# Softcapped attention and a leaky two-matrix layer: weight norms in groups of four chunks, new priorities in the plan, and an exact statement of transposes

## Chip, core and metric

One core of a Trainium2 chip. The metric is the device time of one execution in microseconds, the median of several runs.

## What is computed

The inputs q, k and v have the shape (4, 12, 448, 64): batches, heads, positions, head size.

```python
scores = scale * q @ k^T                    # scale = 1 / sqrt(64)
scores = cap * tanh(scores / cap)           # cap = 30
attn   = softmax(scores)                    # over the last axis
x      = (attn @ v), heads side by side     # (1792, 768)
h      = x @ w_in                           # w_in (768, 2048)
g      = max(h, 0) + alpha * min(h, 0)      # alpha (2048)
out    = g @ w_out                          # w_out (2048, 768)
```

w_in and w_out come as 64-bit floats, the rest as 32-bit floats.

## The kernel before

Products of full precision are made from 16-bit pieces: a number is scaled by a power of two and split into a high and a low half, and three products (high-high, high-low, low-high) stand for one. Batch 0's attention works with 32-bit products instead, save its last unit.

**Attention.** Heads go in pairs, six pairs a batch. In batch 0 each pair is done in two units (parts of 192 and 256 of its 448 columns); in batches 1 to 3 a pair is one unit (`attention`): load q and k, take their absolute maximum (L693, then `allmax`, a transpose on TensorE, a maximum, and a broadcast back by TensorE), scale and split them (L703, L704), turn them by a DMA transpose (L709), then in blocks of 128 queries, two at a time (`steps`): products S (L724), tanh (L508), maximum (L513), exponent (L520), then scale and split the weights (L381 and L389 into `pw`, three buffers) and turn them by DMA transposes (`turn_split`, L547) into `ptall`, which has three slots for the heads, two of which a pair uses. The PV product (L597) follows, and its result goes to `xring` in eight slots, (6 * batch + pair) mod 8. Pairs 2 to 5 of batch 1 take the slots that batch 0's pairs had.

**Weights.** A matrix has 16 chunks of 128 x 768. A chunk is loaded (L825), converted from 64 to 32 bits by three VectorE operations (`to_f32`, L837, L841, L847) and its norms are taken: six products of the chunk with itself on TensorE (L861), whose maxima VectorE reduces (L866, written by L345 in the trace). `norms` does this for a group of `WG` chunks in one PSUM bank. For w_in, each group then gets its scale (`root2`: `allmax` over the group's columns, L358, L360, L362, L365, then L870, L873, L902), and its chunks are scaled and split (`split_w`). For w_out, the norms are taken by groups too, but one scale for all 16 chunks follows the last group.

**Products.** mm1 of a batch (L741) makes g for 16 chunks of w_in from all six pairs; for batch 0 in the two parts. mm2 (L782) makes the output. Evacuations of both go over ScalarE, VectorE and GpSimd (L381, L751, L375, L386).

**The order.** Nothing is issued as it is written. Every piece of work is given to a `Plan` with a priority, an estimate of its length on each engine that may do it, and the regions it reads and writes. `order` plays this forward in an estimated time: each engine that is free takes the ready item with the lowest priority number. The order that results is what is emitted; each engine then works through its own list in order, and waits on the chip for the true dependences. PSUM banks p0 to p3 are lent by kind: at most three for attention ("a"), three for mm1 and mm2 ("m"), and one for norms and `allmax` ("n"), from the first piece that uses a handle to the last. Where TensorE would stand idle before `FILL_END` of the planned time, the plan gives it a product on the identity whose result nobody reads (L991), which keeps its clock up. The constants at the top are the priorities: `A_S` for the units of batch 0, `B1_P` and `B_S` for the pairs of batches 1 to 3, `ST1_P` for a block of queries within one, `PV_P` for the PV product, `WI_P`, `WI_S`, `WO_P`, `WO_S` for the chunks of the weights (`LD_P`, `LO_P` for their loads), `WT_P`, `WT_S` for the scaling of w_out, `MM_P` for mm1, `EVAC_P` for evacuations. `PEN` and `PEN2` are what VectorE adds to the priority of an item that another engine could do.

Of the kernel before, what the change touches and what calls it, by code (L numbers as in the profile page):

```python
# [26 lines left out]
PD_B = 5  # L27
MQ = 3
AQ = 3
PEN = 422.47  # L30
PEN2 = 365.74
B0_P = -18.88
LD_P = -3.44
LO_P = -170.16
MM_P = 732.81
X_P = 22.66
ST_P = -8.0
ST1_P = 14.53
PV_P = 54.55
QK_P = 1.76  # L40
V_P = 31.8
WI_P = 37.0
WI_S = 4.06
A_S = 12.69
MM1_P = 0.51
WO_P = 95.27
WO_S = 3.65
WT_P = -69.69
WT_S = -13.16
B1_P = 65.06  # L50
B_S = 40.73
EVAC_P = 153.38
LAT = 200.0
START = 1230.0
WINDOW = 4096 / 1.2
FILLS = 1
WG = 2
XI = 1
XO = 1
AI = 1  # L60
# [1 line left out]
PW = 3  # L62
QA = 1.0
VA = 0.5
FILL_END = 398871.32
EXPONENT = 0x7F800000


# [7 lines left out]
class Plan:  # L76
# [15 lines left out]
    def op(self, prio, times, fn, r=(), w=(), rows=1.0, port=True):  # L92
        o = lambda: None
        o.prio, o.times, o.fn, o.rows, o.idx, o.port = prio, times, fn, rows, len(self.ops), port
        o.handles, deps = [], set()
        for write, regions in ((False, r), (True, w)):
            for x in regions:
                if isinstance(x, Handle):
                    if x not in o.handles:
                        o.handles.append(x)  # L100
                        x.ops.append(o)
                    x = (x, 0, 1)
                space, lo, hi = x
                old = self.acc.setdefault(space, [])
                deps.update(e[2] for e in old if e[0] < hi and lo < e[1] and (write or e[3]))
                if write:
                    old[:] = [e for e in old if e[0] < lo or hi < e[1]]
        for write, regions in ((False, r), (True, w)):
            for x in regions:
                space, lo, hi = (x, 0, 1) if isinstance(x, Handle) else x  # L110
                self.acc[space].append((lo, hi, o.idx, write))
        o.deps = len(deps)
        o.next = []
        for d in deps:
            self.ops[d].next.append(o)
        self.ops.append(o)
        return o

    def order(self):
# [32 lines left out]
        def put(o):  # L152
            for e in o.times:
                heapq.heappush(ready[e], (o.prio + ((PEN if "act" in o.times else PEN2) if len(o.times) > 1 and e == "dve" else 0.0), o.idx, o))

# [82 lines left out]
def kernel(  # L238
# [15 lines left out]
    NCH = 4  # L254
# [124 lines left out]
    def scaled(e, o, i, s):  # L379
        if e == "act":  # L380
            nc.scalar.activation(out=o, in_=i, func=AF.Copy, scale=s)  # L381
        else:
            nc.vector.tensor_scalar(out=o, in0=i, scalar1=s, scalar2=None, op0=ALU.mult)
# [14 lines left out]
    def load(prio, dst, src, b, pair, w):  # L398
        op(prio, {"sp": (500, 1900, 1000)}, lambda e: nc.sync.dma_start(out=dst.rearrange("p (h c) -> p h c", h=2),
                                                          in_=heads(src, b, pair)), w=w)  # L400
# [7 lines left out]
    def loads32():  # L408
        for pair in range(NPAIR):
            n = 2 * NCH * D  # L410
            for i, src in ((4, k), (6, q)):
                o = pair % 3 * n
                t = wpair[i + pair // 3].rearrange("p a b -> p (a b)")[:CP, o:o + n]
                raw32[i, pair] = t, (("wp", i + pair // 3), o, o + n)
                load(QK_P + A_S * pair, t, src, 0, pair, [raw32[i, pair][1]])
        vbatch(0)
# [11 lines left out]
    def vbatch(b):  # L428

        u = Unit()  # L430
        vb.append(u)
        t = vam[:, b % 2]
        u.vmx, u.inv, u.s = (t[:, NPAIR + i:NPAIR + i + 1] for i in range(3))
        u.osc, u.tok = small[:, 12 + b:13 + b], ("vam", b % 2)
        prio = V_P if b == 0 else B1_P + (b - 1) * NPAIR * B_S - B_S
        op(prio, {"dve": 30}, lambda e: nc.vector.memset(t[:, :NPAIR], 0.0), w=[(u.tok, 0, 9)])
        for pair in range(NPAIR):
            rv, m = vslot(b, pair)
            v0[b, pair] = rv, m
            load(prio + 0.4 * pair, rv, v, b, pair, [m])  # L440
            op(prio + 0.4 * pair, {"dve": 680}, lambda e, pair=pair, rv=rv: absmax(t[:CP, pair:pair + 1], rv),
               r=[m], w=[(u.tok, pair, pair + 1)], port=False)
        prio += 3
        op(prio, {"dve": 80}, lambda e: nc.vector.tensor_reduce(out=u.vmx, in_=t[:, :NPAIR], axis=AX.X, op=ALU.max),
           r=[(u.tok, 0, 6)], w=[(u.tok, 6, 7)])
        first, *rest = pow2(u.inv, u.s, None)
        allmax(prio, u.vmx, P, [(u.tok, 6, 7)], first, [(u.tok, 7, 9)])
        chain(prio, rest, w=[(u.tok, 7, 9)])
# [35 lines left out]
    def steps(u, prio, n, S_, s_ns, sr_, scale, dma):  # L484
# [3 lines left out]
        for i0 in range(0, nb, 2):  # L488
# [5 lines left out]
            sr = (("S", i % 2), 0, 1)  # L494
            pr = prio + (ST1_P if u.b else ST_P) * i0

# [40 lines left out]
    def turn_split(u, pr, n, c, t, tr, f, fr):  # L537

        w = pws[blk_no[0] % PW]
        wt = [(("pw", blk_no[0] % PW), z, z + 1) for z in range(2)]  # L540
        blk_no[0] += 1
        hi, lo = w[:, :NCH, :CP], w[:, NCH:, :CP]
        op(pr, {"act": 640, "dve": 470}, lambda e: scaled(e, hi, t, f), r=[*tr, fr], w=[wt[0]])
        op(pr, {"dve": 680}, lambda e: split_lo(lo, t, f, hi), r=[*tr, fr, wt[0]], w=[wt[1]])
        for h, rows, cols in spans(n, c):
            full = rows.stop - rows.start == P
            op(pr, {"sp": (1294, 1275, 896) if full else (1225, 1275, 448)}, lambda e, h=h, rows=rows, cols=cols: nc.sync.dma_start_transpose(  # L547
                out=u.pt[h][:, :, cols], in_=w[rows].rearrange("p g k -> p (g k)")),
               r=wt, w=[("pt", u.po[h] + 4 * cols.start, u.po[h] + 4 * cols.stop)])

    def turn_32(u, pr, n, c, t, tr, f, fr):

# [79 lines left out]
    def attention32(part, pair):  # L632
# [3 lines left out]
        o, n = PART[part]  # L636
        prio = A_S * (u.idx + 1) + B0_P * part
        ktr = ("tall", pair * S, (pair + 1) * S)
# [30 lines left out]
        if dma:  # L669
            h = PV_split(u, prio + X_P, n, *split_v(u, prio, vt, vr))  # L670
        else:
            h = PV_32(u, prio + X_P, n, vt, vr)
        if dma:
            xout(u, prio + X_P, h, n, o, 1 / P_TOP)
        else:
            xout(u, prio + X_P, h, n, o, vb[0].s, [(vb[0].tok, 7, 9)])


    def attention(b, pair):
        u = Unit()  # L680
        u.b, u.pair, u.idx = b, pair, unit_no[0]
        unit_no[0] += 1
        prio = B1_P + ((b - 1) * NPAIR + pair) * B_S
        n = 2 * NCH * D
# [42 lines left out]
        steps(u, prio, S, S_, lambda c: 430 if c == 3 else 380, [qt], [sc, amt], True)  # L727
        h = PV_split(u, prio + PV_P, S, vs, vt)
        xout(u, prio + PV_P, h, S, 0, 1 / P_TOP)

    grn = [0]

    def mm1(b, j, o, n, prio):
# [13 lines left out]
        grn[0] += 1  # L747
        pr = EVAC_P + prio * 1e-4
        sgt = [("sg", 0, 1)]
# [25 lines left out]
    def mm2(b, t, hf, prio):  # L775
# [10 lines left out]
        for part in range(4):  # L786
# [7 lines left out]
        osc = vb[b].osc if t < 3 else joint[:, b // 2:b // 2 + 1]  # L794
        op(EVAC_P + prio * 1e-4, either(NH, True), lambda e: scaled(e, osb[:, cols], ps_p[h.slot][:, :NH], osc),
           r=[h, *oscs], w=[osr], port=False)
# [6 lines left out]
        for rows in [out_rows(b, t * P, P)] if t < 3 else [out_rows(b - 1, 3 * P, QP), out_rows(b, 3 * P, QP)]:  # L803
            for t0, m, dst in rows:
                op(EVAC_P, {"sp": (500, 1100, 800)}, lambda e, p=p, m=m, dst=dst: nc.sync.dma_start(
                    out=dst[:, a], in_=osb[p:p + m, a]), r=[osr])
# [80 lines left out]
    def w_in_chunks(j0, n):  # L887

        flats = []
        for j in range(j0, j0 + n):  # L890
            prio = WI_P + WI_S * j
            if j + 2 < NF:
# [3 lines left out]
            flats.append((flat, fr))  # L896
            load_w(prio + LD_P, flat, fr, j % 4, src_wi(j), True)
            to_f32(prio, j % 4, flat, fr, share(j, XI))
# [7 lines left out]
    def w_out_all():  # L906
        for j in range(NF):
            prio = WO_P + WO_S * j
            load_w(prio + LO_P, room[j], room_r(j), WO_STAGE[j], src_wo(j), False)
            to_f32(prio, WO_STAGE[j], room[j], room_r(j), share(j, XO))  # L910
            if j % WG == WG - 1:
                js = range(j - WG + 1, j + 1)
                norms(prio, [(room[i], room_r(i)) for i in js], n_wo[:, js[0]:j + 1], ("n_wi", js[0], j + 1))
        root2(WT_P, s_wo, ("s_wo", 0, 1), n_wo, ("n_wi", 0, NF), [wo_scales])
        for j in range(NF):
            split_w(WT_P + WT_S * j, wo[j], room_r(wo_room[j]), room[j], room_r(j), s_wo[:, j:j + 1], ("s_wo", 0, 1), share(j, AO))

# [29 lines left out]
    def out_scale(b):  # L947
# [4 lines left out]

        op(WT_P + 1, {"dve": 150}, scale, r=[(vb[b].tok, 7, 9), ("s_wo", 0, 1)], w=[(("osc", b), 0, 1)])

    def mm1_batch(b, o, n, part):
        for j in range(NF):
            mm1(b, j, o, n, MM_P + 1000 * 2 * b + MM1_P + 10 * part + 0.1 * j)

# [7 lines left out]
    def all_ops():  # L966
        loads32()
        g_scales(30)
        for part in range(2):
            for pair in range(NPAIR):  # L970
                attention32(part, pair)
        for j in range(0, NF, WG):
            w_in_chunks(j, WG)
        for part in range(2):
# [17 lines left out]

    plan.fill, plan.fill_until = fill, FILL_END
    nc.sync.dma_start(out=capt, in_=cap.to_broadcast([P, 1]))
# [44 lines left out]
```

## Time and profile before

| | |
|---|---|
| median of 3 runs | 758.37 us (757.72 to 758.9) |
| profiled execution | 758.37 us, span 756.6 us |
| TensorE busy | 729.0 us, 96% |
| VectorE, ScalarE, GpSimd busy | 510.4, 452.1, 153.7 us |
| mean granted clock of TensorE | 0.988 |

The span goes from the first to the last instruction; the rest of the time lies around it. A granted clock of 1 is 2.4 GHz, of 0.5 is 1.2 GHz; a mean in between is a mixture of the two levels. Busy TensorE includes the fill products.

### The profile page before, as it was taken

To read this page: it belongs to the slowest core of one execution; us is meant where nothing else is said; L and a number is where in the kernel's file an instruction comes from. 1 tells how busy PE (TensorE), PEld (TensorE's weight loads), DVE (VectorE), ACT (ScalarE), POOL (GpSimd) and SP (SyncE) were. 2 spreads that over 40 slices of the span, in tenths; PEclk is the share of its full clock that TensorE was granted. 3 is DMA by queue.
4 is the path that set the end of the run, shared out by engine and by line. 5 is a ranking of instruction groups with operands and counts; after the bars stand their busy time and mean duration, and the time that the engine had idled before them with its cause. 6 is when DMAs were issued, how large, how long until landed. Compare 5 with 4: busy or idle time off the path is not lost.

```text
span 756.6 us, 13862 instructions
## 1 busy us (share of the span) xinstructions
PE 729.0 (96%) x5237; PEld 456.6 (60%) x5237; DVE 510.4 (67%) x1039; ACT 452.1 (60%) x897; POOL 153.7 (20%) x292
## 2 busy tenths in 40 slices
PE   9999999869899999999999999999999999999997
PEld 5766676658788655676545555555555555555664
DVE  3788899998877977777788777877887432443000
ACT  4768888845658966666685666777668531332010
POOL 1211112222344221121443210123343000000000
PEclk9999999987999999999999999999999999999999
DMA  8964545748875649999557799997755660000001
GB/s 204 279 182 130 160 130 139 208 131 200 187 128 98 108 106 203 180 189 171 110 90 143 153 185 191 194 176 144 126 119 96 127 119 1 22 1 1 21 22 42
DMA packets 227938, 98.70 MB, mean 130 GB/s; under 512 B 191456, under 2 KB 224160, under 8 KB 227872
## 3 DMA queue, kind: packets, MB, share of 16 engines
q1 hardware_dynamic: 227872, 97.82, 62.2%
q8 instruction: 41, 0.67, 0.4%
q14 instruction: 25, 0.20, 0.1%
HBM read 45.82 MB, written 5.51 MB: 68 GB/s over the span
## 4 chain that ended last, share of the span: by engine, by line
PE 52%; DMA 5%; DVE 1%; ACT 1%; issue 1%; SPq 0%; POOL 0%; ACTq 0%; DVEq 0%
PE p L741 22%; PE p L782 20%; PE s L724 4%; PE p L597 4%; DMA ptall<-pw 3%; DMA qkTs<-nat 2%; PE p L991 1%; DMA rqk<-in_k_dram 1%; DVE pw L389 0%; PE p L365 0%; SPq L547 0%; ACT nat L381 0%; DVE mxs L513 0%; ACT tall L520 0%; ACT tall L508 0%
## 5 line engine op out<-in xcount | busy, mean ns | idle before, releaser
L741 PE MATMUL p<-xring,wi 128*128 128x448 f16 (+2 forms) x1440 | 230.4, 320 | 5.8 <-DVE xring L389 3.9
L782 PE MATMUL p<-wp,gall 128*128 128x384 f16 x1344 | 225.2, 326 | 0.0
L741 PEld LDWEIGHTS <-wi 128*128 128x128 f16 x1440 | 138.4, 100 | 92.5 <-issue 10.2
L782 PEld LDWEIGHTS <-gall 128*128 128x128 f16 x1344 | 130.0, 98 | 89.6 <-issue 4.3
L520 ACT ACTIVATE tall<-tall,mxs,small 128x448 f32<-128x448 f32 x126 | 94.3, 750 | 17.6 <-POOL mxs L515 15.9
L389 DVE SCALAR_TENSOR_TENSOR pw<-tall,rr,pw 128x448 f16<-128x448 f32 x126 | 85.3, 689 | 19.1 <-ACT pw L381 18.7
L381 ACT ACTIVATE pw<-tall,rr 128x448 f16<-128x448 f32 x100 | 64.8, 662 | 55.6 <-DMA ptall<-pw 40.4
L515 POOL TENSOR_SCALAR mxs<-mxs,small 128x2 f32<-128x2 f32 (+1 forms) x93 | 48.0, 517 | 225.8 <-DVE mxs L513 190.1
L386 POOL TENSOR_TENSOR gall<-gr,gall 128x384 f16<-128x384 f32 (+4 forms) x80 | 64.6, 815 | 131.4 <-ACT gall L375 80.9
L751 DVE SCALAR_TENSOR_TENSOR gr<-p,ca_g,gr 128x448 f32<-128x448 f32 (+2 forms) x80 | 46.8, 585 | 46.0 <-ACT gr L381 45.4
L513 DVE TENSOR_REDUCE mxs<-tall 128x2 f32<-128x896 f32 (+1 forms) x72 | 68.7, 959 | 12.0 <-ACT tall L508 11.6
L508 ACT ACTIVATE tall<-s,ams 128x896 f32<-128x896 f32 (+1 forms) x72 | 64.5, 904 | 10.5 <-PE s L724 4.4
L724 PE MATMUL s<-qkTs 128*128 128x448 f16 (+1 forms) x288 | 60.0, 356 | 4.7 <-DMA qkTs<-nat 3.7
L381 ACT ACTIVATE gr<-p,cs_g 128x448 f32<-128x448 f32 (+2 forms) x54 | 28.8, 533 | 48.0 <-PE p L741 47.1
L375 ACT ACTIVATE gall<-gr 128x384 f16<-128x384 f32 (+4 forms) x83 | 34.8, 433 | 35.0 <-DVE gr L751 34.8
L525 POOL TENSOR_SCALAR rr<-sums 128x2 f32<-128x2 f32 (+1 forms) x96 | 30.2, 315 | 114.2 <-ACT tall L520 82.1
L381 ACT ACTIVATE wp<-p,small 128x384 f32<-128x384 f32 x21 | 12.2, 579 | 59.5 <-PE p L782 59.5
L597 PE MATMUL p<-ptall,vs 112*64 112x448 f16 (+1 forms) x456 | 46.2, 350 | 1.0 <-DMA ptall<-pw 1.0
L991 PE MATMUL p<-ident 128*128 128x128 f16 x695 | 43.2, 223 | 1.7 <-POOL ident masks.py:199 1.7
L991 PEld LDWEIGHTS <-ident 128*128 128x128 f16 x695 | 40.9, 100 | 4.1 <-POOL ident masks.py:199 1.7
L724 PEld LDWEIGHTS <-qkTs 128*128 128x128 f16 (+1 forms) x288 | 21.7, 100 | 28.1 <-issue 9.9
L666 PE MATMUL s<-tall,qkTs 128*128 128x448 f32 x84 | 35.8, 551 | 1.2 <-ACT gall L508 1.2
(141 smaller groups left out, 844.7 us busy)
## 6 DMA issues: line engine op xcount, KB each, us to landing
wp<-in_moe_w_in_dram SPq DMA_DIRECT2D x16, 768.0 KB, 4.9
wp<-in_moe_w_out_dram SPq DMA_DIRECT2D x16, 768.0 KB, 4.7
rvs<-in_v_dram SPq DMA_DIRECT2D x38, 224.0 KB, 3.2
rqk<-in_q_dram SPq DMA_DIRECT2D x18, 224.0 KB, 3.2
rqk<-in_k_dram SPq DMA_DIRECT2D x18, 224.0 KB, 3.5
ptall<-pw SPq DMA_TRANSPOSE x148, 3.3
wp<-in_k_dram SPq DMA_DIRECT2D x6, 224.0 KB, 7.8
wp<-in_q_dram SPq DMA_DIRECT2D x6, 224.0 KB, 7.7
```

Of the source, the lines that this page charges most:

```text
L381: nc.scalar.activation(out=o, in_=i, func=AF.Copy, scale=s)
L386: (nc.gpsimd if e == "pool" else nc.vector).tensor_tensor(out=o, in0=a, in1=b, op=ALU.subtract)
L389: nc.vector.scalar_tensor_tensor(out=o, in0=i, scalar=s, in1=hi, op0=ALU.mult, op1=ALU.subtract)
L508: op(pr, {"act": 245 + 377 * m}, lambda e, s=s, t=t, m=m: nc.scalar.activation(out=t, in_=s[:, :m, :S].rearrange("p c (j k) -> p c j k", j ...
L513: op(pr, {"dve": 136 + 469 * m}, lambda e, mt=mt, t=t: nc.vector.tensor_reduce(out=mt, in_=t, axis=AX.XY, op=ALU.max), r=tr, w=[mr], port= ...
L515: op(pr, {"dve": 200, "pool": 440}, lambda e, mt=mt: (nc.gpsimd if e == "pool" else nc.vector).tensor_scalar(out=mt, in0=mt, scalar1=ncap, ...
L520: nc.scalar.activation(out=t[:, x], in_=t[:, x], func=AF.Exp, scale=capt, bias=mt[:, x:x + 1], accum_out=u.sums[:, c:c + 1])
L597: nc.tensor.matmul(pv[x * D:(x + 1) * D, :n], vs[:, z, c:c + D], u.pt[x][:CP, y * NCH + kc], start=(i == 0), stop=(i == len(prods) - 1))
L724: nc.tensor.matmul(s[rows], qT[:, x * S + cols.start:x * S + cols.stop], qkT[:, r0:r0 + NCH, :], start=(z == 0), stop=(z == 1))
L741: nc.tensor.matmul(ps_p[h.slot][:, :n], w[:, z, kk, :], x[:, d, o:o + n], start=(kk == 0 and z == d), stop=(kk == NPAIR - 1 and z == 1))
L782: nc.tensor.matmul(ps_p[h.slot][:, :NH], g[j][:, d, t * P:(t + 1) * P], w[:, z, hf * NH:(hf + 1) * NH], start=(j == 0 and z == d), stop=(j ...
L991: nc.tensor.matmul(ps_p[slot][:, :P], ident.bitcast(F16)[:, :P], ident.bitcast(F16)[:, P:], start=True, stop=True)
```

## The change

`WG` goes from 2 to 4, so that `norms` and, for w_in, `root2` take four chunks at a time. The priorities get other values. In `turn_split`, the region that a DMA transpose writes is stated to the plan as the eight strips that it writes, where it was stated as one block of a head's region. `FILL_END` is lower.

```diff
--- before.py
+++ after.py
@@ -27,34 +27,34 @@
 PD_B = 5
 MQ = 3
 AQ = 3
-PEN = 422.47
-PEN2 = 365.74
-B0_P = -18.88
-LD_P = -3.44
-LO_P = -170.16
-MM_P = 732.81
-X_P = 22.66
-ST_P = -8.0
-ST1_P = 14.53
-PV_P = 54.55
-QK_P = 1.76
-V_P = 31.8
-WI_P = 37.0
-WI_S = 4.06
-A_S = 12.69
-MM1_P = 0.51
-WO_P = 95.27
-WO_S = 3.65
-WT_P = -69.69
-WT_S = -13.16
-B1_P = 65.06
-B_S = 40.73
-EVAC_P = 153.38
+PEN = 593.1
+PEN2 = 357.34
+B0_P = -21.6
+LD_P = -4.13
+LO_P = -146.94
+MM_P = 766.13
+X_P = 30.7
+ST_P = -12.3
+ST1_P = 9.3
+PV_P = 53.98
+QK_P = -5.54
+V_P = 27.5
+WI_P = 31.8
+WI_S = 4.16
+A_S = 12.4
+MM1_P = 6.26
+WO_P = 75.25
+WO_S = 5.62
+WT_P = -127.9
+WT_S = -15.47
+B1_P = 46.83
+B_S = 32.07
+EVAC_P = 201.2
 LAT = 200.0
 START = 1230.0
...
 FILLS = 1
-WG = 2
+WG = 4
 XI = 1
 XO = 1
 AI = 1
@@ -62,7 +62,7 @@
 PW = 3
 QA = 1.0
 VA = 0.5
-FILL_END = 398871.32
+FILL_END = 365429.37
 EXPONENT = 0x7F800000
 
 
@@ -546,7 +546,7 @@
             full = rows.stop - rows.start == P
             op(pr, {"sp": (1294, 1275, 896) if full else (1225, 1275, 448)}, lambda e, h=h, rows=rows, cols=cols: nc.sync.dma_start_transpose(
                 out=u.pt[h][:, :, cols], in_=w[rows].rearrange("p g k -> p (g k)")),
-               r=wt, w=[("pt", u.po[h] + 4 * cols.start, u.po[h] + 4 * cols.stop)])
+               r=wt, w=[("pt", u.po[h] + (g_ * n + cols.start) / 2, u.po[h] + (g_ * n + cols.stop) / 2) for g_ in range(2 * NCH)])
 
     def turn_32(u, pr, n, c, t, tr, f, fr):
 
```

## Rows read from the trace of the kernel before

**Rows 1.** Windows: from:to us, length, PE PEld DVE ACT POOL busy (xcount), PEclk, DMA, GB/s.
```profile
25.00:100.00 75.00, 73.72 (x525) 50.58 (x523) 61.78 (x129) 57.36 (x121) 10.85 (x28) 1.00 0.63 177
125.00:175.00 50.00, 37.35 (x316) 29.90 (x314) 46.79 (x91) 34.37 (x76) 11.51 (x21) 0.90 0.68 182
175.00:238.00 63.00, 60.26 (x563) 49.73 (x561) 48.77 (x99) 40.28 (x90) 25.20 (x38) 0.95 0.75 152
238.00:250.50 12.50, 12.50 (x196) 11.07 (x196) 11.10 (x25) 11.03 (x20) 4.38 (x4) 1.00 0.53 103
250.50:314.80 64.30, 62.81 (x406) 35.80 (x404) 50.33 (x94) 47.00 (x85) 11.07 (x23) 1.00 0.80 151
314.80:348.70 33.90, 32.79 (x490) 27.93 (x489) 26.00 (x61) 22.14 (x44) 7.22 (x14) 1.00 1.09 192
348.70:642.00 293.30, 292.13 (x1784) 157.06 (x1782) 206.52 (x412) 183.58 (x359) 72.20 (x138) 1.00 0.72 133
```

**Rows 2.** The same view of the fill products alone (L991); the sum is of all stretches.
```profile
238.00:250.50 12.50, 9.66 (x167) 9.41 (x168) 1.00 0.53 103
...
314.80:348.70 33.90, 24.57 (x418) 23.67 (x417) 1.00 1.09 192
348.70:642.00 293.30, 0.16 (x3) 0.00 (x0) 1.00 0.72 133
...
sum 756.60, PE 43.17 PEld 40.89; mean PE 4.32 PEld 4.09
```

**Rows 3.** The chain that ended last: start us, us, what.
```profile
332.83 0.31 PE p L365 x2
...
343.68 2.39 PE p L597 x24
...
348.86 3.40 PE p L741 x18
...
353.02 0.10 PE p L362
```

**Rows 4.** Groups of instructions: line, engine, operation, shapes, count, busy us, mean ns, idle before.
```profile
L513 DVE TENSOR_REDUCE mxs<-tall 128x2 f32<-128x896 f32 x54 | 57.9, 1077 | 10.8 <-ACT tall L508 10.5
...
L847 DVE SCALAR_TENSOR_TENSOR wp<-wp,wp 128x768 int32<-128x768 int32 x18 | 17.2, 959 | 0.0
...
L513 DVE TENSOR_REDUCE mxs<-tall 128x1 f32<-128x448 f32 x18 | 10.9, 606 | 1.2 <-ACT tall L508 1.1
...
L837 DVE TENSOR_SCALAR wp<-wp 128x768 int32<-128x768 int32 x18 | 9.8, 545 | 1.8 <-DMA wp<-in_moe_w_out_dram 1.8
...
L360 DVE TENSOR_SCALAR mxt<-ident,mxt 2x2 f32<-2x2 f32 x26 | 7.8, 299 | 0.9
...
L345 DVE TENSOR_REDUCE n_wi<-p 128x2 f32<-128x256 f32 x16 | 6.7, 418 | 4.4 <-PE p L861 4.4
...
L358 DVE TENSOR_REDUCE mxt<-p 2x1 f32<-2x128 f32 x8 | 2.2, 276 | 3.0 <-PE p L362 3.0
...
L873 DVE TENSOR_SCALAR iv_wi<-iv_wi 128x2 f32<-128x2 f32 x8 | 1.2, 156 | 0.0
```

**Rows 5.** TensorE in order of time: start us, us, instruction.
```profile
175.26 0.85 PE L861 MATMUL p<-wp 128*128 128x128 bf16 x6
...
189.78 0.52 PE L861 MATMUL p<-wp 128*128 128x128 bf16 x6
...
195.88 0.26 PE L362 MATMUL p<-ident,small 112*2 112x112 f32 x1
...
216.67 0.51 PE L861 MATMUL p<-wp 128*128 128x128 bf16 x6
...
232.75 0.51 PE L861 MATMUL p<-wp 128*128 128x128 bf16 x6
```

**Rows 6.** TensorE's longest wait, 100 to 350 us: us in total, times, longest.
```profile
PE p L741 <- DVE xring L389: 3.9, 1, 3.9
```

**Rows 7.** Waits of SyncE's queue, 180 to 230 us: us in total, times, longest.
```profile
SPq L547 <- DVE gr L751: 11.8, 3, 5.3
```

## Prediction

> **What bounds the kernel now.** Read first the busy times by stretch, cut where TensorE's work changes [rows 1]. TensorE is busy for 729.0 us of the 756.6 us span, but this is not 729.0 us of wanted work: 43.17 us are fill products on the identity, which the plan puts in where it finds TensorE free [rows 2]. What is left, 685.9 us, is the floor that no order of the work can go under, give or take what the clock costs. So the question for any new order is how much of the 27.6 us of idle and of the 43.2 us of fills it can remove. The rows of the fills and of the stretches say where these are: 12.65 us of plain idle at 125 to 175 us, where the granted clock also falls to 0.90 in the mean; 9.66 us of fills at 238 to 250.5; 24.57 us of fills at 314.8 to 348.7. After that TensorE is full: 292.13 of 293.30 us up to 642 us, with 0.16 us of fills. Everything that can be won lies ahead of 348.7 us.
>
> Then the chain of waits says what ends the last hole [rows 3]. The first product of mm1 of batch 1 starts at 348.86 us. Just ahead of it stands the last PV product of batch 1's attention (343.68 us) with fills on either side. mm1 reads all six pairs' columns, so it waits for the last pair. Behind it TensorE never waits again, so each microsecond by which batch 1's attention ends earlier is a microsecond off the end, until the holes are used up. The hole at 238 to 250.5 has another cause: mm1 of batch 0 is done and w_out isn't scaled yet.
>
> What is late in batch 1's attention? From 175 to 348.7 us VectorE is busy for 48.77 + 11.10 + 50.33 + 26.00 = 136.2 of 173.7 us, a share of 0.784, ScalarE for less [rows 1]. In 125 to 175 us VectorE has 46.79 of 50, a share of 0.936. So there VectorE is the bound, and what goes first on it matters; later the pairs wait for one another (a pair of heads takes two of three slots of transposed weights, and pairs 2 to 5 may write their columns only after mm1 of batch 0 has read the old ones). A pair that comes to 175 us further along loses less there.
>
> **The change part by part.**
> *Groups of four.* For w_in, 8 groups become 4. Each group that goes takes with it a maximum over a transposed column (276 ns), the diagonal (299), and three small VectorE operations on its columns, of which one is shown (156 each) [rows 4]: 1.04 us. Four groups: 4.2 us of VectorE. The reductions of the norms halve in number and double in width. None of 512 columns from PSUM was run; the nearest rows are the 448- and 896-wide maxima, 606 and 1077 ns, so 1.05 ns for a column more; 256 columns more make 418 + 269 = 687 ns. At the least it costs nothing more (418), at the most twice (836). With 687, 8 x 418 - 4 x 687 = 0.6 us is saved for w_in, and as much for w_out. In all 5.4 us of VectorE's 510.4 us. On TensorE a group takes a transpose and a broadcast, 0.10 and 0.31 us of its time by the chain [rows 3]; four of them are 1.6 us. They fall at 25 to 125 us, where TensorE has little left (73.72 of 75 us at 25 to 100). I take 1.6 us there as the gain of this edit (bounds 0, if the plan only puts fills in its place, and 5.4, if all of VectorE's part counted), and don't add VectorE's: most of it falls ahead of the stretch in which VectorE is full.
>
> *What the group delays.* The first chunk of a group now waits for three others before it is scaled. A chunk takes one conversion step of 545 ns and two of about 959 on VectorE [rows 4], 2.5 us, so two more chunks are 5 us of VectorE and more where other work comes between. For w_out this is nothing: the one scale of all sixteen chunks waits for the last chunk either way. For w_in it costs nothing as long as mm1 reaches a chunk later than that, since the product over part 0 stands behind all attention products in priority; without this cover it is 5 us a group, once.
>
> *The bank.* A group keeps its PSUM bank from its first product to its reduction, and only one such handle may be live; the maxima of the attention's q and k use the same kind. By the norm products of w_out, six a chunk, the second last four chunks lie at 175.26 to 189.78 us and the last four at 216.67 to 232.75 (the first and last of each four are shown) [rows 5], so a hold would be 14.5 and 16.1 us instead of the length of a pair. The only q and k maximum near them, at 195.88 us, falls between the two. So 0 with these times, up to 16.1 us if the new order puts such a maximum into a hold. I take 0 for the sum, as the row lies outside both holds, and keep 16.1 for the range. The Trainium skill (Perfetto Trace Analysis, Optimization Strategy) says that a gap that repeats on the engine that should be full can mean that too little SBUF or PSUM is there for the next tile. By that rule a bank held longer can only hurt, and the sum would come out 8.0 us higher, half a hold. This trace doesn't bear it out so far: the longest idle of TensorE at 100 to 350 us is a wait for a column of xring, 3.9 us [rows 6], no bank.
>
> *The priorities.* Lower goes first. Batch 1's pair p stood at 65.1 + 40.7p and stands at 46.8 + 32.1p: 18 earlier at pair 0, 62 at pair 5. Its blocks of queries follow every 2 x 14.5 = 29 and now 2 x 9.3 = 18.6. w_out's chunk j stood at 95.3 + 3.65j and stands at 75.3 + 5.62j. So the last blocks of pair 0 went behind all 16 chunks (152 against 150) and now go behind 5 (103 against 75 to 98): 11 chunks of 2.5 us, some 27 us of VectorE, no longer stand ahead of them. For pair 1's last blocks it is 16 and now 11. mm1's evacuations move from 153 to 201, so pairs 3 and 4 go ahead of them. Batch 0 (12.7 a unit, now 12.4) keeps its place. The work isn't less by this. What it can do is to fill VectorE's idle after 175 us. Bounds: its share stays at 0.784, and nothing is won; or it rises to the 0.936 of 125 to 175 us, and 136.2 us of work take 145.5 us, 28.2 us less. Between them I take the share of 25 to 100 us, where attention and conversions also run side by side: 61.78 / 75 = 0.824, so 165.3 us, 8.4 us less. It is nearer to the lower end because the waits behind one another, for slots and columns, stay.
>
> What is late next: w_out is spread further (its last chunk at 160 instead of 150), so mm2 of batch 0 starts later and its 9.66 us of fills may grow. That costs nothing as long as attention still ends last; the products of mm2 are then done later, not lost.
>
> *The plan's exact statement of transposes.* A transpose was stated as one block of a head's region, and now as the eight strips it writes. The instruction and its true dependences are the same. Between units of one size both state the same waits, as the PV product reads the whole region. It differs only where batch 1 takes over from batch 0. I take 0; the bounds are 11.8 us either way, the time in which SyncE's queue stood in front of a transpose behind mm1's evacuations at 180 to 230 us [rows 7].
>
> *Fills end at 365 instead of 399 us of the plan's time.* After 348.7 us there are 0.16 us of them [rows 2]: 0. If a hole moved behind that point, its idle would come without fills, and the clock would fall as it does at 125 to 175 us.
>
> Sum: 1.6 + 8.4 = 10.0 us. The profiled execution took 758.37 us (the span and 1.8 us around it), which is the median of the runs too: 748.4 us.
>
> **The rivals.**
> *Nothing to measure (757 us).* The holes change places: attention ends earlier, w_out later, and VectorE's share stays 0.784. Only the 1.6 us are left. For it: VectorE's total work before 348.7 us is nearly the same. Against: with 0.78 it isn't work but order that sets the stretch. That the exact statement changes no order at all belongs here too.
>
> *Far more (728 us).* The share reaches 0.936: 758.4 - 1.6 - 28.2 = 728.6. Against: the slots and columns that make pairs wait are as few as before, and DMA has a share of 1.09 in the last hole [rows 1].
>
> *Slower (765 us).* One mechanism: the q and k maximum of pair 1 or 2 comes to lie inside a hold of four w_out chunks, which now go behind attention's work and so take longer to complete. With half a hold in place of the 8.4 us: 758.4 - 1.6 + 8.0 = 764.8; a whole one makes 772.9. It decides once the wait is over 10 us. For it: w_out's spacing grows from 3.65 to 5.62, so holds grow by half. Against: the row at 195.88 us.
>
> **How the numbers follow.** The forecast (739 to 756) has 0.45, far more 0.13, nothing 0.18, slower 0.24. A measurement here can tell 0.2%, 1.5 us, from no change. Of "nothing" 0.06 lies below 756.9; of "slower" 0.02 lies within 0.2%. So faster 0.64, same 0.14, slower 0.22. The range goes from 730, which leaves out most of "far more", to 767, which leaves out the whole holds, together not over 0.2. The likeliest case alone is 739 to 756.
>
> **What would show it.** Right: 8 group reductions of 512 columns, near 0.69 us; the first mm1 product of batch 1 near 339 us; fills down from 43 to some 33 us; VectorE's share from 175 us to that product near 0.82. Wrong: the last PV product of batch 1 at 344 us or later; a q and k maximum that follows right on a group's reduction; idle without fills after 350 us; a longer stretch of half clock at 125 to 175 us.

## Result: 751.2 us against 758.1, and the profile after

The changed kernel takes 751.19 us in the median of four runs (749.35 to 752.13), the kernel before 758.05 on the same chips. The ratio is 0.9896, 95% interval 0.987 to 0.9921: 1.0% faster. The profiled execution took 750.85 us with a span of 749.1, against 758.37 and 756.6.

The busy times by stretch, cut again where TensorE's work changes (columns as in [rows 1]):

```profile
25.00:100.00 75.00, 73.37 (x539) 50.48 (x538) 63.53 (x126) 54.49 (x114) 12.67 (x27) 0.98 0.63 189
100.00:150.00 50.00, 46.78 (x385) 35.76 (x385) 44.82 (x81) 41.81 (x86) 9.56 (x19) 1.00 0.50 135
150.00:250.90 100.90, 81.67 (x746) 65.28 (x743) 87.56 (x165) 71.48 (x154) 35.48 (x52) 0.93 0.82 172
250.90:277.40 26.50, 26.12 (x335) 21.14 (x334) 24.99 (x49) 22.61 (x38) 10.04 (x9) 1.00 0.57 104
277.40:332.10 54.70, 54.70 (x352) 30.75 (x349) 41.25 (x93) 33.64 (x64) 7.59 (x17) 1.00 0.83 163
332.10:341.70 9.60, 9.60 (x147) 8.38 (x145) 8.80 (x23) 9.00 (x21) 1.43 (x5) 1.00 0.73 167
341.70:642.00 300.30, 300.00 (x1825) 161.72 (x1823) 210.50 (x415) 185.92 (x366) 75.70 (x136) 1.00 0.72 133
```

The fill products alone (as in [rows 2]):

```profile
250.90:277.40 26.50, 15.46 (x256) 14.62 (x255) 1.00 0.57 104
...
332.10:341.70 9.60, 6.91 (x121) 6.74 (x120) 1.00 0.73 167
341.70:642.00 300.30, 0.18 (x4) 0.01 (x1) 1.00 0.72 133
...
sum 749.10, PE 33.98 PEld 31.40; mean PE 3.78 PEld 3.49
```

And TensorE in order of time where the last hole ends:

```profile
332.14 2.12 PE L991 MATMUL p<-ident 128*128 128x128 f16 x35
334.18 2.79 PE L597 MATMUL p<-ptall,vs 112*64 112x448 f16 x24
336.91 4.97 PE L991 MATMUL p<-ident 128*128 128x128 f16 x86
341.72 3.57 PE L741 MATMUL p<-xring,wi 128*128 128x448 f16 x18
```

Read the last rows first. mm1 of batch 1 starts at 341.72 us, where it started at 348.7 by the same view (348.86 in the chain of [rows 3]); the last PV product stands at 334.18 instead of 343.68, again between fills. From the start of mm1 to the end it is 407.4 us, and was 407.9. So the whole difference of the spans, 7.5 us, is made ahead of that product, up to half a microsecond. The last hole has shrunk from 24.57 us of fills to 6.91; the one ahead of mm2 of batch 0 has grown from 9.66 to 15.46, and mm2 starts at 264.4 instead of 250.9 us. In sum fills went from 43.17 to 33.98 us (9.2 less), idle from 27.6 to 749.1 - 718.3 = 30.8 (3.2 more), and the wanted work from 685.9 to 684.4 us (1.5 less): 7.5 together. The idle has moved forward too. Up to some 251 us, the first row before and the second after:

```profile
0.00:250.50 250.50, 231.00 (x1931) 173.65 (x1932) 203.18 (x417) 178.26 (x376) 62.87 (x117) 0.97 0.66 166
0.00:250.90 250.90, 225.13 (x1800) 166.28 (x1801) 207.26 (x396) 179.49 (x376) 61.84 (x119) 0.97 0.71 174
```

There it went from 19.5 to 25.8 us (6.3 more), and behind it fell by 3.1. The granted clock of the stretch is 0.97 both times.

VectorE's share from 175 us to that product, in the changed kernel:

```profile
125.00:175.00 50.00, 42.20 (x383) 33.42 (x381) 43.69 (x83) 38.40 (x85) 13.13 (x23) 0.97 0.63 148
175.00:341.70 166.70, 153.50 (x1388) 109.53 (x1386) 140.37 (x287) 119.05 (x232) 45.65 (x72) 0.97 0.80 159
```

140.37 of 166.70 us is 0.842; it was 0.784. The stretch has 4.2 us more VectorE work than before, as 125 to 175 us has 3.1 less (0.874 instead of 0.936).

The group's own instructions (line, engine, operation, shapes, count, busy us, mean ns, idle before):

```profile
L345 DVE TENSOR_REDUCE n_wi<-p 128x4 f32<-128x512 f32 x8 | 5.5, 688 | 3.3 <-PE p L861 3.2
...
L358 DVE TENSOR_REDUCE mxt<-p 4x1 f32<-4x128 f32 x4 | 1.1, 273 | 0.7 <-PE p L362 0.6
```

There are 8 reductions of 512 columns at 688 ns, where there were 16 of 256 at 418 [rows 4].

### The profile page after: what moved, and what is told of

It is laid out like the page before. It is cut to its first block, busy times and chain, and to the rows that moved or that the text cites. A ratio compares the mean times of both kernels' runs of the same rounds, so it can differ in the third digit from the quotient of the medians.

```text
span 749.1 us, 13417 instructions
## 1 busy us (share of the span) xinstructions
PE 718.3 (96%) x5043; PEld 446.5 (60%) x5043; DVE 514.4 (69%) x1021; ACT 450.0 (60%) x893; POOL 156.6 (21%) x286
## 4 chain that ended last, share of the span: by engine, by line
PE 83%; DMA 8%; DVE 5%; ACT 2%; issue 1%; POOL 0%; SPq 0%; ACTq 0%; POOLq 0%
PE p L782 27%; PE p L741 25%; PE s L724 6%; PE p L597 5%; DMA ptall<-pw 4%; PE p L561 4%; PE s L666 4%; PE p L991 4%; DMA qkTs<-nat 3%; PE p L611 2%; PE p L455 2%; PE p L454 1%; PE p L861 1%; PE p L365 1%; DVE wi L389 1%
## 5 line engine op out<-in xcount | busy, mean ns | idle before, releaser
L389 DVE SCALAR_TENSOR_TENSOR pw<-tall,rr,pw 128x448 f16<-128x448 f32 x126 | 88.0, 716 | 17.7 <-ACT pw L381 16.8
L386 POOL TENSOR_TENSOR gall<-gr,gall 128x192 f16<-128x192 f32 (+4 forms) x76 | 63.5, 845 | 124.7 <-ACT gall L375 83.8
L515 POOL TENSOR_SCALAR mxs<-mxs,small 128x2 f32<-128x2 f32 (+1 forms) x90 | 44.5, 495 | 212.8 <-DVE mxs L513 161.6
L751 DVE SCALAR_TENSOR_TENSOR gr<-p,ca_g,gr 128x448 f32<-128x448 f32 (+2 forms) x80 | 46.9, 587 | 49.6 <-ACT gr L381 48.9
L513 DVE TENSOR_REDUCE mxs<-tall 128x2 f32<-128x896 f32 x72 | 68.5, 961 | 5.1 <-ACT tall L508 4.5
L381 ACT ACTIVATE gr<-p,cs_g 128x448 f32<-128x448 f32 (+2 forms) x59 | 32.7, 554 | 58.0 <-PE p L741 53.9
L525 POOL TENSOR_SCALAR rr<-sums 128x2 f32<-128x2 f32 (+1 forms) x96 | 35.2, 367 | 118.4 <-ACT tall L520 87.6
L666 PE MATMUL s<-tall,qkTs 128*128 128x448 f32 x84 | 37.3, 570 | 1.2 <-ACT gall L508 1.2
L597 PEld LDWEIGHTS <-vs 112*64 112x64 f16 x456 | 25.9, 110 | 18.8 <-issue 5.5
L991 PE MATMUL p<-ident 128*128 128x128 f16 x513 | 34.0, 226 | 2.8 <-POOL ident masks.py:199 1.7
```

Source lines behind the costliest of these rows:

```text
L386: (nc.gpsimd if e == "pool" else nc.vector).tensor_tensor(out=o, in0=a, in1=b, op=ALU.subtract)
L389: nc.vector.scalar_tensor_tensor(out=o, in0=i, scalar=s, in1=hi, op0=ALU.mult, op1=ALU.subtract)
L513: op(pr, {"dve": 136 + 469 * m}, lambda e, mt=mt, t=t: nc.vector.tensor_reduce(out=mt, in_=t, axis=AX.XY, op=ALU.max), r=tr, w=[mr], port= ...
L597: nc.tensor.matmul(pv[x * D:(x + 1) * D, :n], vs[:, z, c:c + D], u.pt[x][:CP, y * NCH + kc], start=(i == 0), stop=(i == len(prods) - 1))
L666: steps(u, prio, n, lambda s, c: nc.tensor.matmul(s, qz[:, c * P:(c + 1) * P], kt[:, pair], start=True, stop=True), lambda c: 750, [qr, kt ...
L991: nc.tensor.matmul(ps_p[slot][:, :P], ident.bitcast(F16)[:, :P], ident.bitcast(F16)[:, P:], start=True, stop=True)
```

## The experiments

In this case each edit changes the order in which the plan emits the work, so each kernel below is one complete order. Two of the edits change nothing: with the old or the new statement of the transposes' regions, and with `FILL_END` at 398.9 or 365.4, the lists of instructions of all engines are the same, one by one (the statement tried with the priorities before and with those after, `FILL_END` with those after). What is left of the change is `WG` and the priorities. All ratios are to the kernel before on the same chip, with their 95% intervals.

**Groups alone, and priorities alone.** The first is the kernel before with

```diff
-WG = 2
+WG = 4
```

> The kernel before with groups of four and nothing else. If the priorities made the gain, the groups alone are worth their removed work: 756 to 757 us, with the first mm1 product of batch 1 at 347 to 349 us. If the groups made it: 750 to 753 us, and that product near 342. If a longer hold of the bank costs more than the groups save: over 760 us.

Measured: 763.21 us, ratio 1.0076 (1.0051 to 1.010). Slower. The second is the kernel after with

```diff
-WG = 4
+WG = 2
```

> The kernel after with groups of two again. If the priorities made the gain: 752 to 753 us, first mm1 product of batch 1 at 342 to 344 us. If the groups made it: 757 to 759 us. If the two only work together, as the new priorities suit four chunks and no other number: slower than 760 us.

Measured: 793.13 us, ratio 1.0458 (1.0437 to 1.0479). Each part by itself loses; together they win 1.0%. The terms of the prediction, 1.6 us for the one and 8.4 for the other, can't be had one by one.

A place where groups alone lose is seen in TensorE's list of that run, at the last four chunks of w_out (start us, us, instruction):

```profile
208.54 0.51 PE L861 MATMUL p<-wp 128*128 128x128 bf16 x6
218.11 0.51 PE L861 MATMUL p<-wp 128*128 128x128 bf16 x6
222.39 0.51 PE L861 MATMUL p<-wp 128*128 128x128 bf16 x6
233.85 0.51 PE L861 MATMUL p<-wp 128*128 128x128 bf16 x6
236.91 0.27 PE L362 MATMUL p<-ident,n_wi 128*16 128x128 f32 x1
239.62 0.26 PE L362 MATMUL p<-ident,small 112*2 112x112 f32 x1
```

The last line is the q and k maximum of pair 2. It stood at 195.88 us before [rows 5], ahead of the hold; now it comes behind the hold of 208.54 to 233.85 us and behind the maximum for w_out's scale. The PV product of pair 2 follows at 292.20 us, where it stood at 279.68, and mm1 of batch 1 starts at 354.8.

**A second handle for norms and maxima.** To test this, the plan lends two such handles at once:

```diff
-        limit = {"a": AQ, "m": MQ, "n": 1}
+        limit = {"a": AQ, "m": MQ, "n": 2}
```

With groups alone:

> Groups of four alone, but the plan lends two handles of the kind for norms and maxima at once instead of one. If groups alone lost time because the q and k maximum of pair 2 stood behind a hold of four chunks (239.6 us there, 195.9 before): that maximum comes back to 200 us or earlier, and the time to 752 to 757 us. If they lost it through the order of anything else: within 2 us of the 763.2 us of groups alone.

Measured: 760.3 us, ratio 1.0024 (1.0003 to 1.0044), so about 4 of the 5.8 us are back; the two intervals don't touch. But this order's output is wrong, by a relative error of 0.047, and why is open; so its time is a hint and no proof. TensorE's list shows the maximum of pair 2 ahead of its place above:

```profile
201.59 0.34 PE L362 MATMUL p<-ident,small 112*2 112x112 f32 x1
...
286.33 2.46 PE L597 MATMUL p<-ptall,vs 112*64 112x448 f16 x24
```

The PV product of pair 2 is earlier by 5.9 us. It missed the 752 to 757 us that were expected: by this hint the hold is some two thirds of the loss, and the rest isn't settled.

In the kernel after:

> The kernel after with two such handles. Its q and k maximum of pair 3 follows right on the last hold (254.0 us after 210.6 to 250.1). If this hold still costs: 740 to 749 us, with the PV product of pair 3 before 290 us. If pair 3 waits for something else there, or if two handles take banks that mm1 needs: 751 us or more.

Measured: 769.14 us, ratio 1.0136 (1.0103 to 1.0169). The expected gain fell out. TensorE's list of this run, and VectorE's:

```profile
220.34 0.26 PE L362 MATMUL p<-ident,small 112*2 112x112 f32 x1
...
270.13 2.46 PE L597 MATMUL p<-ptall,vs 112*64 112x448 f16 x24
...
292.57 4.00 PE L741 MATMUL p<-xring,wi 128*128 128x256 f16 x18 [10.38 <-DVE gr L751]
```

```profile
297.16 0.61 DVE L389 SCALAR_TENSOR_TENSOR xring<-p,xring 128x448 f16<-128x448 f32 x1
```

The maximum of pair 3 does come earlier, at 220.34 instead of 254.02 us. But now the PV product of pair 2 starts at 270.13, ahead of the last product of mm1 of batch 0 at 292.57, whose inputs lie in the column slot that pair 2 is to write. Its second half is written at 297.16 us; until then it keeps its bank, 27 us, and within this time TensorE stands idle for 10.38 us. That wait is for an evacuation (L751), and VectorE's list shows what stood ahead of it:

```profile
274.69 0.48 DVE L751 SCALAR_TENSOR_TENSOR gr<-p,ca_g,gr 128x256 f32<-128x256 f32 x1
275.08 3.90 DVE L389 SCALAR_TENSOR_TENSOR wp<-wp,s_wo,wp 128x768 f16<-128x768 f32 x3
...
290.17 1.95 DVE L389 SCALAR_TENSOR_TENSOR wp<-wp,s_wo,wp 128x768 f16<-128x768 f32 x2
292.03 0.48 DVE L751 SCALAR_TENSOR_TENSOR gr<-p,ca_g,gr 128x256 f32<-128x256 f32 x1
```

Between these two evacuations VectorE scales w_out (`wp<-wp,s_wo`) for 13.2 of 16.9 us. Its priority (`WT_P`) puts it ahead of evacuations in every order here. So two things meet in the gap, a kept bank and the scaling of w_out, and this run doesn't say which of them made it. Nor does it say what the hold of four chunks costs the kernel after, as the second handle changed the rest of the order with it.

**Evacuations.** The priorities-alone run shows both things larger. Its PV products of pairs 2 and 3, its evacuations of mm1 (both L751), and the writes of the pairs' results:

```profile
273.72 4.48 PE L597 MATMUL p<-ptall,vs 112*64 112x448 f16 x24 [1.22 <-DVE ams L338]
299.14 2.46 PE L597 MATMUL p<-ptall,vs 112*64 112x448 f16 x24
```

```profile
247.51 0.47 DVE L751 SCALAR_TENSOR_TENSOR gr<-p,ca_g,gr 128x256 f32<-128x256 f32 x1
273.58 0.48 DVE L751 SCALAR_TENSOR_TENSOR gr<-p,ca_g,gr 128x256 f32<-128x256 f32 x1
```

```profile
318.89 0.62 DVE L383 TENSOR_SCALAR xring<-p 128x448 f16<-128x448 f32 x1
320.02 1.15 DVE L389 SCALAR_TENSOR_TENSOR xring<-p,xring 128x448 f16<-128x448 f32 x2
```

For 26 us no product of mm1 is evacuated. In this time, which ends before pair 2's product, VectorE scales w_out for more than half (the group's row of 248 to 273.6 us):

```profile
L389 DVE SCALAR_TENSOR_TENSOR wp<-wp,s_wo,wp 128x768 f16<-128x768 f32 x15 | 14.7, 1009 | 0.4 <-ACT wp L381 0.4
```

The rest is mostly attention, of which pairs 3 and 4 now go ahead of evacuations, as pair 2 did. What these pairs finish can't be written until mm1 is done: pair 2 waits from 273.72 to 318.89, pair 3 from 299.14, each with a bank. mm1 of batch 0 ends at 320.3 us instead of 238. But most of TensorE's idle comes ahead of this: the first row is the time without an evacuation, the second the time in which pair 2's bank is kept.

```profile
247.98:273.58 25.60, 9.77 (x89) 6.51 (x86) 23.61 (x36) 22.64 (x36) 4.83 (x5) 0.75 0.50 93
273.72:318.89 45.17, 39.22 (x293) 28.94 (x293) 37.29 (x82) 34.43 (x75) 17.42 (x31) 0.88 0.82 163
```

TensorE is idle for 15.8 of 25.6 us in the first and for 6.0 of 45.2 us in the second. With the old rank of evacuations and nothing else changed in this run:

```diff
-EVAC_P = 201.2
+EVAC_P = 153.38
```

> The new priorities with groups of two, and only the evacuations' priority as before (153 instead of 201). If the 793 us of priorities alone come from evacuations of mm1 that stand behind pairs whose finished products can't be written before mm1 is done: 750 to 762 us, with mm1 of batch 0 done by 255 us. If they come from the groups of two: over 780 us.

Measured: 756.05 us, ratio 0.997 (0.9948 to 0.9993): 37 us come back with one number, so the rank of evacuations is what makes this order so slow. mm1 of batch 0 ends at 280.6 us, later than the 255 that were expected, but now ahead of the PV product of pair 2 at 286.15. So it is late here without any pair's bank being kept for it; w_out's scaling begins ahead of its end in this order too, at 251.7 us. The same edit in the kernel after:

> The kernel after with the evacuations' priority as before. If their later place is part of the gain: 754 to 760 us. If it is a risk that groups of four happen to escape: 746 to 752 us, mm1 of batch 0 done before 250 us.

Measured: 754.46 us, ratio 0.9945 (0.9927 to 0.9964). So the later rank of evacuations, which costs 37 us with groups of two, gains with groups of four, by 0.5%; the intervals lie apart. With the old rank, groups of four against groups of two are 754.46 against 756.05, in overlapping intervals. And between:

```diff
-EVAC_P = 201.2
+EVAC_P = 178.0
```

> The kernel after with evacuations at 178, between pair 4 and pair 5 of batch 1, where 153.4 gave 754.5 us and 201.2 gave 751.2 us. If the rank of evacuations among the pairs moves the time smoothly: 751 to 755 us. If mm1 of batch 0 falls behind the PV product of pair 2, as in the run with priorities alone: over 760 us.

Measured: 759.75 us, ratio 1.0017 (0.9995 to 1.0038). Neither expectation: it isn't smooth, and mm1 of batch 0 ends at 251.8 us, ahead of pair 2's PV product at 259.2. What is late here is the last pairs: PV at 322.3 and 341.7 us (pairs 4 and 5) instead of 316.0 and 334.2.

**Attention's and w_out's priorities.**

```diff
-ST1_P = 9.3
-B1_P = 46.83
-B_S = 32.07
+ST1_P = 14.53
+B1_P = 65.06
+B_S = 40.73
```

> The kernel after with the three priorities of batches 1 to 3 (start, spacing of pairs, spacing of blocks) as before. If attention that goes earlier made the gain: 757 to 760 us, last PV product of batch 1 at 343 us or later. If the weights' priorities or the groups made it: 750 to 753 us.

Measured: 758.62 us, ratio 0.9999 (0.998 to 1.0018). All of the gain is gone. But the pairs aren't what is late at first: PV of pairs 0 and 1 at 209.9 and 232.0 us, earlier than in the kernel after (217.3 and 241.1). Pair 2's product comes at 271.86, ahead of mm1's end at 282.4, and its second half is written at 282.67. The last PV product comes at 336.89, not at the 343 or later that were expected, and still no time is won: from 320 us to the start of mm1 of batch 1 at 343.7 TensorE is full of wanted work, with no fills. The reverse, these three values in the kernel before:

> The kernel before with only these three priorities as after. If attention that goes earlier makes the gain by itself: 750 to 753 us, with the last PV product of batch 1 near 335 us. If it needs the later place of w_out and the evacuations: 755 to 760 us.

Measured: 761.36 us, ratio 1.0037 (1.002 to 1.0055), slower than either expectation. Pairs 0 and 1 are earlier than before (211.9 and 238.7 against 228.4 and 244.6), and pair 2 is later (288.4 against 279.7). Then w_out in the kernel after:

```diff
-WO_P = 75.25
-WO_S = 5.62
+WO_P = 95.27
+WO_S = 3.65
```

> The kernel after with the two priorities of w_out's chunks (start and spacing) as before, so that w_out is converted sooner relative to batch 1. If w_out's later place buys the earlier attention: 754 to 759 us, mm2 of batch 0 starting by 255 us and the last PV product at 338 us or later. If it only delays mm2: 747 to 750 us.

Measured: 753.92 us, ratio 0.9933 (0.9913 to 0.9953). Between the two expectations; mm2 of batch 0 starts at 263.7 us, hardly sooner, and the last PV product comes at 335.9.

**Small steps.** What do steps that should be worth nothing do?

```diff
-B1_P = 46.83
+B1_P = 47.83
```

> The kernel after with batch 1 starting one unit of priority later (47.83 instead of 46.83), a step that by the argument of the priorities is worth next to nothing. If the earlier place of attention as such makes the gain: 750 to 753 us. If the gain hangs on one particular order out of many: anywhere from 751 to 770 us.

Measured: 762.83 us, ratio 1.0045 (1.0024 to 1.0066).

```diff
-WI_P = 31.8
+WI_P = 32.8
```

> The same test at another place: the kernel after with the chunks of w_in one unit later (32.8 instead of 31.8). Earlier attention as such: 750 to 753 us. One order out of many: anywhere from 751 to 770 us.

Measured: 761.09 us, ratio 1.0033 (1.002 to 1.0047). Both lose all of the gain and more, by 10 us and above against the kernel after. The run with `B1_P` at 47.83 shows what has changed: pair 2's PV product and, on VectorE, its write:

```profile
258.14 2.46 PE L597 MATMUL p<-ptall,vs 112*64 112x448 f16 x24
...
275.04 8.33 PE L741 MATMUL p<-xring,wi 128*128 128x256 f16 x72 [0.15 <-DVE gr L751]
```

```profile
283.52 0.62 DVE L389 SCALAR_TENSOR_TENSOR xring<-p,xring 128x448 f16<-128x448 f32 x1
```

It has its product at the time of the kernel after (257.75), but mm1 of batch 0 ends at 283.4 instead of 250.3, and the bank is kept for 25 us. w_out's scaling begins at 255.3 us, as in the kernel after (255.6), where mm1 was done by then.

All orders side by side, from their profiled executions, in us; the ratio is that of all runs, from whose median the profiled one lies up to 3 us away. The fourth column is where the first instruction of w_out's scaling starts:

| order | ratio | mm1 of batch 0 ends | w_out's scaling begins | PV of pair 2 | PV of pair 5 | mm1 of batch 1 starts | from there to the end |
|---|---|---|---|---|---|---|---|
| before | 1 | 238.0 | 241.8 | 279.7 | 343.6 | 348.7 | 407.9 |
| after | 0.9896 | 250.3 | 255.6 | 257.8 | 334.2 | 341.7 | 407.4 |
| after, w_out as before | 0.9933 | 251.2 | 254.3 | 256.1 | 335.9 | 344.1 | 408.1 |
| after, evacuations 153 | 0.9945 | 254.1 | 259.0 | 258.2 | 339.4 | 343.8 | 408.7 |
| priorities, evacuations 153 | 0.997 | 280.6 | 251.7 | 286.2 | 343.4 | 348.3 | 406.9 |
| after, attention as before | 0.9999 | 282.4 | 229.9 | 271.9 | 336.9 | 343.7 | 410.7 |
| after, evacuations 178 | 1.0017 | 251.8 | 257.1 | 259.2 | 341.7 | 348.7 | 407.2 |
| groups, two handles | 1.0024 | 262.6 | 236.8 | 286.3 | 346.1 | 351.0 | 406.7 |
| after, w_in + 1 | 1.0033 | 290.1 | 261.9 | 253.5 | 344.2 | 350.7 | 408.8 |
| before, attention as after | 1.0037 | 261.3 | 261.2 | 288.4 | 345.6 | 351.6 | 406.7 |
| after, start + 1 | 1.0045 | 283.4 | 255.3 | 258.1 | 343.0 | 348.9 | 409.1 |
| groups alone | 1.0076 | 237.1 | 240.7 | 292.2 | 349.9 | 354.8 | 405.3 |
| after, two handles | 1.0136 | 296.6 | 272.5 | 270.1 | 345.0 | 363.5 | 403.5 |
| priorities alone | 1.0458 | 320.3 | 244.8 | 273.7 | 348.4 | 386.5 | 404.7 |

The last column hardly moves: from the first product of mm1 of batch 1 every order takes 403.5 to 410.7 us. In the five orders with the PV product of pair 2 ahead of mm1's end, the pair's bank is kept, and none is faster than the kernel before. The three with a ratio under 0.995 have both ends early: pair 2 at 256 to 258 us, and mm1 done a few microseconds before. The order with evacuations at 178 has both too and isn't faster; so this goes with the gain in these runs and isn't enough for it.

The kept bank isn't shown to be what costs these five their time. While pair 2's bank is kept, TensorE is idle for 0 us (attention as before), 4.2 (start + 1), 6.0 (priorities alone), 11.8 (w_in + 1) and 12.7 (two handles), and there is a rival. The same five orders, and two more (priorities with evacuations at 153, groups with two handles), have w_out's scaling begin well before mm1 of batch 0 ends. It is some 30 us of ScalarE and VectorE together, the engines that evacuate mm1, and it goes ahead of evacuations. None of these seven has a ratio under 0.997. No run here changes the rank of the scaling alone, so how much of the losses is the bank's and how much the scaling's stays open.

## Why the prediction was right, point by point

**What bounds the kernel: right for the kernel after, and not for every order.** The start of mm1 of batch 1 sets the time in all 14 orders. But it waits for the last pair, as the prediction has it, only while there are holes. In six orders (the five above and priorities with evacuations at 153) TensorE has less than 1 us of fills from 320 us to that start, and mm2 of batch 0 takes their place. In two of them the last pair isn't the end at all: mm1 starts 35 us (priorities alone) and 16 us (two handles) after the last PV product, behind mm2. For priorities alone:

```profile
350.00:386.50 36.50, 36.50 (x247) 20.78 (x243) 27.53 (x57) 26.67 (x50) 5.47 (x14) 1.00 0.84 158
```

The floor of 685.9 us of wanted work was to hold "give or take what the clock costs", and that is not little: with groups alone, at a mean granted clock of 1.00 instead of 0.988, wanted work is 739.4 - 64.3 = 675.1 us.

**The groups: right in their instructions, wrong as a term.** The 512-wide reduction took 688 ns (687 was worked out), a group's maximum 273 (276). Wanted TensorE work fell by 1.5 us in all (1.6 for the groups), but as the clock alone moves it by more than that, this agreement shows little. That 1.6 us are won by groups of themselves doesn't hold: alone they cost 5.8. VectorE's whole busy time rose from 510.4 to 514.4 us instead of falling by 5.4.

**What the group delays: right** that the single scale of w_out isn't put off by a longer group; in the groups-alone order mm2 starts at 250.2 us and mm1 of batch 0 ends at 237.1, both as before.

**The bank: 0 isn't contradicted in the kernel after, and the price shows elsewhere.** In the changed kernel the last hold and its neighbours are:

```profile
207.00 0.26 PE L362 MATMUL p<-ident,small 112*2 112x112 f32 x1
210.55 0.51 PE L861 MATMUL p<-wp 128*128 128x128 bf16 x6 [0.25 <-DVE ams L338]
...
250.14 0.51 PE L861 MATMUL p<-wp 128*128 128x128 bf16 x6
251.70 0.27 PE L362 MATMUL p<-ident,n_wi 128*16 128x128 f32 x1
254.02 0.26 PE L362 MATMUL p<-ident,small 112*2 112x112 f32 x1
```

It lasts 39.6 us, not 16.1. Pair 2's maximum slips through at 207.00, just ahead of it; pair 3's comes right behind it at 254.02, which the prediction named as a sign of being wrong, though about where it stood before (254.75). What that costs no run shows. In the groups-alone order pair 2's didn't slip through. That is the rival "slower", as it was described, and it came out at 763 us where 765 was worked out, with the two-handle run as the only hint that the hold is its cause. The Trainium skill's rule that a repeated gap can mean too little PSUM (Perfetto Trace Analysis, Optimization Strategy) isn't borne out by the trace of before, and these runs don't settle it: pair 2's bank is kept for 11 to 45 us in five of them, but the one wait over 5 us that falls into such a time, 10.38 us with two handles, is also one in which VectorE scales w_out.

**The priorities: the size was near, the step as it was argued fell.** VectorE's share rose from 0.784 to 0.842 (0.824 was taken), and the stretch took 166.7 us (165.3). But the argument was that earlier attention fills VectorE's idle. Attention's first two pairs are earlier than before, by up to 16.5 us, in nine of the ten orders that have its new priorities, and six of the ten are not faster than before; with the old ones in the kernel after, they are as early. That batch 0 keeps its place and the rest follows was the weak step: mm1 of batch 0 and pair 2 race for a column slot, and the sum had no term for a pair that is too early. The waits "for slots and columns" were named as a reason for taking less, not as a loss; and that w_out's scaling can come ahead of mm1's evacuations has no term either.

**What is late next: right.** mm2 of batch 0 starts 13.5 us later, its hole grew by 5.8 us, and attention still ended last.

**The exact statement and the end of fills: 0, shown** by identical lists of instructions, so the 11.8 us that were kept as its bounds weren't needed.

**The sum.** 10.0 us were forecast; the medians differ by 6.9, the spans by 7.5. The start of mm1 moved by 7.0 (near 339 us was forecast, 341.7 measured), fills by 9.2 (10). What is missing is the 3.2 us of new idle, to which the sum gave no term. It isn't the longer stretch of half clock that was named among the signs of a wrong forecast: the clock at 125 to 175 us is 0.97, and was 0.90. TensorE's longest waits in the changed kernel, 100 to 342 us:

```profile
PE p L741 <- DVE gr L751: 5.8, 3, 3.7
PE p L861 <- DVE wp L847: 4.6, 2, 3.5
PE s L724 <- ACT gall L375: 3.9, 1, 3.9
```

The first isn't the price of the later rank of evacuations: with the old rank in the kernel after it is 7.8 us, and before, mm1 waited about as long in all (1.9 us for evacuations and 3.9 for a column of xring). The third, a product S behind a conversion of g on ScalarE, wasn't among the waits before. No run tests it, so what makes the new idle stays open.

That the time fell into the likeliest case is in part luck. Neither term is won by itself, and two steps of one unit, which the argument counts as nothing, take the whole gain away. The chance of 0.64 for faster was right for this order. Of the twelve other orders that were timed, three are faster by over 0.2% and seven slower; as most of them undo a part of the change, this is no measure of the chance, but it says how little the argument knows of one order.

**Open.** Whether the kept bank or w_out's scaling slows mm1 of batch 0 in the slower orders; why the order with evacuations at 178 loses 7.5 us at its last pairs; the remaining 2 us, and the wrong output, of groups with two handles; and what in groups of four lets mm1 of batch 0 get ahead under the new priorities (part 0 of it is done by 195 us with groups of four and by 237 with groups of two, with w_in's last chunks scaled at about the same time).

## What to carry to other kernels

In a kernel whose order comes from a plan, an edit's own cost says little about its time: test the edits together and one by one, and shake the order with steps that should be worth nothing, to see whether a gain belongs to the idea or to one order. Work that is moved earlier can be too early: a result that can't be written yet keeps its PSUM bank until others have read its destination. So look, for each piece that goes ahead, at who must have read its destination, and at what else goes ahead of the evacuations that those readers need.

## What was not expected of the hardware

The split of the attention weights on VectorE (L389 into pw, 128 x 448, 126 times) took 689 ns in the mean before and 716 after, the same instruction on the same shapes; that alone is 2.7 us of VectorE (85.3 and 88.0). Why was not tried.
